# Second layer of a two-layer MLP chain: seven block products instead of eight in the second matmul, for three of a tile's four groups

## The chip, the cores and the metric

One core of a Trainium2 chip runs the kernel alone. The metric is device time in microseconds (us) of one execution. The kernel before was timed in three runs, and one further execution was profiled.

## The reference

Linear attention makes x of 4608 tokens by 512. Two MLP layers follow, each 512 to 2048 to 512; only their activations differ:

```python
x = attention(q, k, v)                     # 4608 x 512
h = x @ w_in;  r = np.maximum(h, 0.0)      # first layer, 512 x 2048
x = (r * r) @ w_out                        # 2048 x 512
h = x @ w_in;  g = h * np.cos(h)           # second layer
out = g @ w_out
```

All of it is float32. The kernel gets that accuracy from fp32r matmuls by splitting each operand into a high and a low part (`h` by a cast, `l` by a subtraction) and running three matmuls per product: high by high, high by low, low by high. The weights arrive as float64 words and are converted on the chip.

## The kernel before

**Two phases.** In the first (up to 497 us on the profile's clock) the attention runs, and beside it the first layer with its first 1024 hidden units, one chunk after the other (`run_chunks`). In the second, `run_slots` does the rest. Its unit is a **slot** `(m, t, q)`: layer m (0 or 1), token tile t (four of 1024 tokens and one of 512, each as two halves j of `ht` = 512 or 256 tokens) and group q of 512 hidden units. Layer 0 has two groups left per tile, layer 1 has four: 10 + 20 slots.

**First products of a slot.** `first_product` (L457) computes the 2 x 2 blocks of h from the 2 x 2 blocks of x and w_in in seven block products of 12 matmuls instead of eight (the Strassen-Winograd scheme), 84 matmuls with 512 columns (256 in the small tile). They go alternately to the PSUM tiles FA and FB; `keep` (ScalarE), `add` (VectorE) and `last` (ScalarE) drain them, each before the product after next may write the same tile. The seven combinations of x come from `x_block`, once per tile, those of w_in are made at conversion time and lie in DRAM (`wi_d`).

**Activation.** Layer 1 takes h times cos h in five steps, `cos_1` to `cos_5` (ScalarE, VectorE, ScalarE, ScalarE, VectorE), then `g_hi` (ScalarE) and `g_lo` (VectorE) split the result, block by block.

**Second products.** `second` (L555) multiplies g by w_out without block tricks. In layer 1 that is 96 matmuls of 512 columns per slot (48 in the small tile): 8 output units of 128 tokens, 4 chunks of 128 hidden units, three matmuls each. Four units share the PSUM tiles SA and SB (two banks each), and `drain` (L579) empties a tile into the SBUF tile `sum`: ScalarE copies for a tile's group 0, VectorE adds for the others. After the last group `sum` goes out.

**Order.** `run_slots` interleaves: after each first product matmul, as many second ones as are due. The second products of slot k start at position `k + LAG2` with LAG2 = 1.12, in units of one slot's 84 first matmuls. Loads, drains and activation steps are jobs at positions of their own (`at(pos(...), ...)`), and a scheduler of the framework orders the instructions of each engine from that. An engine works through its instructions in order.

**Buffers.** `w_p` holds 16 tiles of 4 KB per partition: loaded `wi` and `wo`, the `sum` tiles, and in the slots also the high parts `wh` of weights being converted (`conv_w`, L143). The pool `c` holds 18 tiles for h, y and g. All loads and stores of the slots are issued by SyncE.

**Conversion.** `load_w`/`conv_w` take 24 items of kind "out" (w_out, 8 of layer 0 and 16 of layer 1) and 24 of kind "pair" (w_in), on a timetable (`w_items`): the "out" items during the first phase, the 16 "pair" items of layer 1 between slots 0.5 and 8.4.

Of the kernel before, what the change touches and what calls it, by code (L numbers as in the profile page):

```python
# [8 lines left out]
F32 = mybir.dt.float32  # L9
# [13 lines left out]
def kernel(  # L23
# [77 lines left out]
    def as32(ap):  # L101
        return ap.bitcast(F32)
# [40 lines left out]
    def conv_w(kind, m, f, i):  # L143
        raw = raws.pop((kind, m, f, i))
        if kind == "pair":
# [10 lines left out]
            l = a.bitcast(F32R)[:, 1:]  # L156
            nc.scalar.copy(out=h, in_=a[:, 1:])  # L157
            nc.vector.tensor_tensor(out=l, in0=a[:, 1:], in1=as32(h[:]), op=ALU.subtract)
            q, pp = divmod(f - first_pair[m], 2)
            for k, x in enumerate((h[:], l)):  # L160
                nc.sync.dma_start(out=wi_d[m, q][:, :, k, pp, i, :], in_=as32(x))
# [383 lines left out]
    def sum_tile(k, n):  # L545
        m, t, q = slots[k]
        j, i = units(k)[2 * n]
        t0, ht = TILES[t]
        if q == 0:
            sums[m, t, n] = e = w_p.tile([P, 2, 512], F32, tag="w", name="sum")  # L550
            if m == 0:
                for b, s0, done, size in pieces(t0 + j * ht, ht, TOK):
                    nc.sync.dma_start(out=e[:, :, done:done + size], in_=p_d[b][:, i:i + 2, s0:s0 + size])

    def second(k, n):  # L555
        m, t, q = slots[k]
# [22 lines left out]
    def drain(k, n):  # L579
        m, t, q = slots[k]  # L580
        t0, ht = TILES[t]
        j, i = units(k)[2 * n]
        ps = psum[("SA", "SB")[n % 2]]
        e = sums[m, t, n]
        if m == 0:
            e, ps = e[:, :, :ht], ps[:, :, :ht]
        if q or m == 0:
# [3 lines left out]
        if q < groups_of[m][-1]:  # L591
            return
        if m == 0:
            nc.sync.dma_start(out=y_d[t][:, j, i:i + 2, :], in_=e)
        else:
            r = t0 + j * ht + i * P
            nc.sync.dma_start(out=out[r:r + 2 * P, :].rearrange("(a p) d -> p a d", p=P), in_=e)
# [11 lines left out]
    def pos(slot):  # L609
        return nA0 + slot + 0.002  # L610
# [18 lines left out]
    def outs_of(m, ps):  # L629
        return [("out", m, f, 1) for p in ps for f in (2 * p, 2 * p + 1)]  # L630

    def pairs_in(m, ps):
        return [("pair", m, p, i) for p in ps for i in range(2)]

    w_items, w_at = [], []
    for fs, n, step in ((range(2), -14, 0.1), (range(2, 6), -2.2, 0.7), (range(6, NH), 4, 0.8)):
# [37 lines left out]
    for k, (m, t, q) in enumerate(slots):  # L674
        if q == 0:
            for a in range(2):
                at(pos(k + (a - 3.6) * PH) if k else nA0 - 6, load_quads, m, t, a)
            for f, i in enumerate(ORDER):
                at(pos(k + (f - 1.9) * PH) if k or f > 2 else nA0 - 4 + f, x_block, k, i)
        for f, i in enumerate(ORDER):  # L680
            at(pos(k + (f - 2.7) * PH) if k or f > 2 else nA0 - 5 + f / 2, load_wi, k, i)
        for a, c in enumerate(CHUNKS):
            at(pos(k + LAG2 - 0.4 + a / 8), load_wo, k, c)
# [7 lines left out]
        chain = (cos_1, cos_2, cos_3, cos_4, cos_5, g_hi, g_lo) if m else (relu_1, relu_2, g_hi, g_lo)  # L691
# [3 lines left out]
        for n in range(len(units(k)) // 2):  # L695
# [24 lines left out]
            run_jobs(n + 0.5)  # L720

    def run_slots():
        seconds = [
            (k + LAG2 + n / len(units(k)) / 12, k, n)
            for k in range(len(slots))
            for n in range(12 * len(units(k)))
        ]
# [27 lines left out]
    with ExitStack() as early:  # L755
# [6 lines left out]
        with tc.tile_pool(name="att", bufs=1, side="right") as att_p:  # L762
# [64 lines left out]
```

## Time and profile before

| | us |
|---|---|
| median of 3 runs (lowest, highest) | 1623.52 (1622.73, 1629.05) |
| the profiled execution | 1623.71 |
| its span, first to last instruction | 1621.6 |
| TensorE (PE) busy | 1589.4 |
| VectorE (DVE) busy | 1056.2 |
| ScalarE (ACT) busy | 947.9 |
| GpSimd (POOL) busy | 81.3 |

The span is 2.1 us shorter than the execution's own time. "PEld" is the weight loading of TensorE, which runs beside the matmuls. Matmuls are pipelined: one is listed with 390 ns, while the next starts 0.23 us after it, so their rate is read from starts, not from durations. The layer-1 slots stand from about 872 us to the end; there TensorE never pauses until the last drain.

### The profile page before, as it was taken

To read this page: it belongs to the slowest core of one execution; us is meant where nothing else is said; L and a number is where in the kernel's file an instruction comes from. 1 tells how busy PE (TensorE), PEld (TensorE's weight loads), DVE (VectorE), ACT (ScalarE), POOL (GpSimd) and SP (SyncE) were. 2 spreads that over 40 slices of the span, in tenths; PEclk is the share of its full clock that TensorE was granted. 3 is DMA by queue.
4 is the path that set the end of the run, shared out by engine and by line. 5 is a ranking of instruction groups with operands and counts; after the bars stand their busy time and mean duration, and the time that the engine had idled before them with its cause. 6 is when DMAs were issued, how large, how long until landed. Compare 5 with 4: busy or idle time off the path is not lost.

```text
span 1621.6 us, 21070 instructions
## 1 busy us (share of the span) xinstructions
PE 1589.4 (98%) x7928; PEld 1305.7 (81%) x7928; DVE 1056.2 (65%) x1410; ACT 947.9 (58%) x1348; POOL 81.3 (5%) x74
## 2 busy tenths in 40 slices
PE   5999999999999999999999999999999999999998
PEld 4777777788887887778789888888888888888887
DVE  7967777787766867565536557645764576456645
ACT  6977777774436645554435656555655555555554
POOL 1102222232000000000000000000000000000000
PEclk9999999999999999999999999999999999999999
DMA  9855787554577988787778544644564455544682
GB/s 323 266 170 176 245 261 242 176 195 150 169 241 268 326 291 283 259 282 247 274 262 291 189 136 166 211 159 131 168 208 169 130 169 181 182 130 155 221 301 90
DMA packets 169572, 344.27 MB, mean 212 GB/s; under 512 B 15360, under 2 KB 92672, under 8 KB 169472
## 3 DMA queue, kind: packets, MB, share of 16 engines
q1 hardware_dynamic: 168704, 340.58, 63.2%
q0 software_dynamic: 768, 2.36, 0.4%
q8 instruction: 63, 1.03, 0.3%
q14 instruction: 37, 0.30, 0.1%
HBM read 270.53 MB, written 72.35 MB: 211 GB/s over the span
## 4 chain that ended last, share of the span: by engine, by line
PE 88%; DMA 5%; DVE 4%; ACT 2%; issue 1%; SPq 1%; POOL 0%; DVEq 0%; POOLq 0%
PE SB L572 17%; PE SA L572 17%; PE FA L467 15%; PE FB L467 15%; PE acc L386 10%; PE l L349 9%; DMA wi_d<-raw 1%; PE o L349 1%; DMA xraw<-x_d 1%; DMA wi<-wi_d 1%; PE ss L349 1%; DMA q<-in_qT 1%; DVE sum L588 1%; PE l L228 0%; PE o L262 0%
## 5 line engine op out<-in xcount | busy, mean ns | idle before, releaser
L467 PE MATMUL FA<-xh,wi 128*128 128x512 f32 (+1 forms) x840 | 304.0, 368 | 1.4 <-issue 1.3
L467 PE MATMUL FB<-xh,wi 128*128 128x512 f32 (+1 forms) x840 | 304.0, 368 | 0.0
L572 PE MATMUL SA<-wo,gh 128*128 128x512 f32 x576 | 223.1, 390 | 0.0
L572 PE MATMUL SB<-wo,gh 128*128 128x512 f32 x576 | 212.1, 390 | 0.0
L467 PEld LDWEIGHTS FA<-xh,wi 128*128 128x128 f32 x840 | 157.8, 188 | 30.6 <-issue 1.7
L508 ACT ACTIVATE y<-h,zerob 128x1024 int32<-128x1024 f32 (+1 forms) x80 | 85.4, 1067 | 164.3 <-DVE h L487 163.7
L467 PEld LDWEIGHTS FB<-xh,wi 128*128 128x128 f32 x840 | 157.8, 188 | 28.2 <-DVE h L491 0.2
L526 DVE SCALAR_TENSOR_TENSOR y<-y,h 128x1024 f32<-128x1024 f32 (+1 forms) x80 | 89.4, 1117 | 95.8 <-ACT y L522 95.8
L572 PEld LDWEIGHTS SB<-wo,gh 128*128 128x128 f32 x576 | 107.9, 188 | 21.9 <-ACT gh L532 0.2
L572 PEld LDWEIGHTS SA<-wo,gh 128*128 128x128 f32 x576 | 108.1, 188 | 21.2
L512 DVE SCALAR_TENSOR_TENSOR y<-y,h 128x1024 f32<-128x1024 int32 (+1 forms) x80 | 89.3, 1116 | 52.5 <-ACT y L508 51.8
L572 PE MATMUL SA<-gh,wo 128*128 128x512 f32 (+1 forms) x320 | 118.2, 372 | 5.0 <-ACT wh L157 2.7
L518 ACT ACTIVATE y<-y 128x1024 f32<-128x1024 f32 (+1 forms) x80 | 78.1, 976 | 62.8 <-DVE y L512 62.8
L536 DVE TENSOR_TENSOR gl<-y,gh 128x1024 fp32r<-128x1024 f32 (+1 forms) x80 | 89.3, 1116 | 38.4 <-ACT gh L532 38.4
L386 PE MATMUL acc<-gh,wh 128*128 128x512 f32 x288 | 113.6, 396 | 0.0
L386 PE MATMUL acc<-gl,wh 128*128 128x512 f32 x288 | 112.9, 392 | 0.0
L386 PE MATMUL acc<-gh,wl 128*128 128x512 f32 x288 | 112.6, 391 | 0.0
L572 PE MATMUL SB<-gh,wo 128*128 128x512 f32 (+1 forms) x320 | 111.5, 370 | 1.1 <-DVE sum L588 1.1
L572 PE MATMUL SB<-wo,gl 128*128 128x512 f32 x288 | 112.4, 390 | 0.0
L572 PE MATMUL SA<-wo,gl 128*128 128x512 f32 x288 | 112.3, 390 | 0.0
L467 PE MATMUL FA<-xl,wi 128*128 128x512 f32 (+1 forms) x300 | 110.5, 368 | 0.0
L467 PE MATMUL FB<-xl,wi 128*128 128x512 f32 (+1 forms) x300 | 110.3, 368 | 0.0
(156 smaller groups left out, 3282.5 us busy)
## 6 DMA issues: line engine op xcount, KB each, us to landing
wi<-wi_d SPq DMA_DIRECT2D x210, 512.0 KB, 4.6
wo<-wo_d SPq DMA_DIRECT2D x120, 512.0 KB, 4.6
kvld<-in_kv SPq DMA_DIRECT2D x32, 512.0 KB, 6.8
raw<-in_wA SPq DMA_DIRECT2D x24, 512.0 KB, 5.3
wi_d<-wh SPq DMA_DIRECT2D x24, 448.0 KB, 3.3
wi_d<-raw SPq DMA_DIRECT2D x24, 448.0 KB, 3.9
q<-in_qT SPq DMA_DIRECT2D x32, 288.0 KB, 4.1
p_d<-ev SPq DMA_DIRECT2D x18, 512.0 KB, 3.7
```

The source lines that it names most:

```text
L349: nc.tensor.matmul(ps, a[:, 0, cs], m[:], start=(c == 0 and k == 0), stop=(c == NKC - 1 and k == 2))
L386: nc.tensor.matmul(o, a[:, cs], m[:], start=(f == 0 and n == 0), stop=(f == NH - 1 and n == 2), skip_group_check=True)
L467: nc.tensor.matmul(ps[:, pp, :], a, b, start=(i in (0, 1, 2) and n == 0), stop=(n == 5), skip_group_check=True)
L508: nc.scalar.activation(out=y.bitcast(I32), in_=hs[k, b], func=AF.Identity, bias=zerob)
L512: nc.vector.scalar_tensor_tensor(out=y, in0=y.bitcast(I32), scalar=-1.0, in1=hs[k, b], op0=ALU.mult, op1=ALU.add)
L518: nc.scalar.activation(out=y, in_=y, func=AF.Sin, scale=math.pi)
L526: nc.vector.scalar_tensor_tensor(out=y, in0=y, scalar=-2.0 * math.pi, in1=hs.pop((k, b)), op0=ALU.add, op1=ALU.mult)
L536: nc.vector.tensor_tensor(out=l, in0=ys.pop((k, b)), in1=as32(h), op=ALU.subtract)
L572: nc.tensor.matmul(ps, lhs, rhs, start=(a == 0 and (x, y) == (0, 0)), stop=last, skip_group_check=True)
L588: nc.vector.tensor_tensor(out=e, in0=ps, in1=e, op=ALU.add)
```

## The change

For groups 0, 1 and 2 of every layer-1 tile (`seven`) the second products become seven block products too. The block form has half as many output columns: each matmul has 256 columns (`second_product`), 24 of them per product, 168 per slot (84 in the small tile) where 96 (48) stood. Group 3 keeps `second`.

- The seven combinations of g are made by `s_block` (four subtractions, then seven casts and seven subtractions, where four of each stood).
- The seven combinations of w_out are made at conversion time (kind "seven") and stored in `ws_d`; `load_ws` loads seven tiles of 512 KB per slot in the place of four `wo`. 12 "out" items go, 12 "seven" items come: 8 in the first phase, 4 among the 16 "pair" items, whose stretch now ends at slot 9.
- Partial products accumulate in SA and SB as in the first products; `drain_product` empties one after each product into four `sum` tiles per token tile (four ScalarE copies and three VectorE adds in group 0, seven VectorE adds in groups 1 and 2). Group 3's drains are split into two adds of 512 elements, since `sum` is laid out by column halves.
- LAG2 goes from 1.12 to 1.25. The `wh` of conversions in the slots come from pool `c` instead of `w_p`; in the first phase they come in two halves from `temp`.

```diff
+    seven = {(1, q) for q in range(NP - 1)}
+    ws_d = {k: dram.tile([P, NPR, 2, 2, 2, P], F32, name=f"ws_d{k[1]}") for k in sorted(seven)}
...
-            p_h, tag = (pools["h"], "w") if pools["h"] is w_p else (pools["h"], "x")
-            h = p_h.tile([P, NPR, P], F32R, tag=tag, name="wh")
...
+            where = [n for n in ("c", "x") if n in pools]
+            if where:
+                parts = [(0, 8, pools[where[0]].tile([P, 8, P], F32R, tag=where[0], name="wh"))]
+            else:
+                parts = [(o, o + 4, temp([P, 4, P], F32R, "wh")) for o in (0, 4)]
...
+    S_ORDER = (0, 2, 3, 4, 5, 1, 6)
...
+    def s_block(k, i):
+        m, t, q = slots[k]
+        b11, b12, b21, b22 = (ys.get((k, b)) for b in ((0, 0), (0, 1), (1, 0), (1, 1)))
...
+        if i == 2:
+            ys[k, "t1"] = minus(t_tile(k, F32, "t"), b12, b11)
+        if i == 3:
+            ys[k, "t2"] = minus(t_tile(k, F32, "t"), b22, ys[k, "t1"])
...
+        gs[k, i] = h, l = [t_tile(k, F32R, f"g{n}") for n in "hl"]
+        nc.scalar.copy(out=h, in_=src)
+        nc.vector.tensor_tensor(out=l, in0=src, in1=as32(h), op=ALU.subtract)
...
+    def s_bank(k, i):
+        return psum[("SA", "SB")[(k + (i in (1, 2, 4))) % 2]]
...
+                    nc.tensor.matmul(
+                        ps[:, b, :],
+                        g[y][:, pp, b * P:(b + 1) * P],
+                        w[:, x, pp, :, :].rearrange("p i n -> p (i n)"),
+                        start=(i in (0, 1, 2) and n == 0 and b % 2 == 0),
+                        stop=(n == 5),
+                        skip_group_check=True,
+                    )
...
+    def drain_product(k, i):
+        m, t, q = slots[k]
+        ps, d, j = blocks_of(t, s_bank(k, i)), *SUM_OF[i]
+        if q == 0 and i in (0, 2, 3, 6):
+            sums[t, d, j] = e = w_p.tile([P, 2, 512], F32, tag="w", name="sum")
+            nc.scalar.copy(out=blocks_of(t, e), in_=ps)
         else:
-            nc.scalar.copy(out=e, in_=ps)
...
+            e = blocks_of(t, sums[t, d, j])
+            nc.vector.tensor_tensor(out=e, in0=ps, in1=e, op=ALU.add)
...
-    LAG2 = 1.12
+    LAG2 = 1.25
...
+        if (m, q) in seven:
+            for f, i in enumerate(S_ORDER):
+                at(pos(k + LAG2 + (f - 2.7) * PH), load_ws, k, i)
+                at(pos(k + LAG2 + (f - 1.6) * PH), s_block, k, i)
+        else:
+            for a, c in enumerate(CHUNKS):
+                at(pos(k + LAG2 - 0.4 + a / 8), load_wo, k, c)
```

**TensorE, a stretch in the middle of layer 1.** In these rows `wi` and `x` belong to first products, `wo`/`ws` and `g` to second ones. Before:

```order
L467 MATMUL FA_5629<-xl_10864,wi_10831 128x512
L572 MATMUL SB_5632<-wo_10681,gl_10549 128x512
L467 MATMUL FA_5629<-xh_10862,wi_10831 128x512
L572 MATMUL SB_5632<-wo_10681,gh_10548 128x512 x2
L467 MATMUL FA_5629<-xh_10862,wi_10831 128x512
```

With the change:

```order
L657 MATMUL SA_5650<-ws_10925,gl_10985 128x256
L488 MATMUL FA_5648<-xh_9917,wi_10890 128x512
L657 MATMUL SA_5650<-ws_10925,gh_10984 128x256 x2
L488 MATMUL FB_5649<-xh_9979,wi_10944 128x512
L657 MATMUL SA_5650<-ws_10925,gl_10985 128x256
```

Between two first matmuls of 512 columns there now stand two second ones of 256, where one of 512 stood most of the time.

**VectorE, the fourth slot of the second layer-1 tile.** L588 and L680 drain second products, L512/L526 and L533/L547 are cosine steps, L536, L557 and L640 make low parts of g, L422/L441 and L438/L457 are the next tile's `x_block`, L622 the new combinations. Before, the first rows after the last `add` of the slot ahead; 26 rows stand between that add and the next of its kind:

```order
L512 SCALAR_TENSOR_TENSOR y_10381<-y_10381,h_10370 128x1024
L536 TENSOR_TENSOR gl_10392<-y_10343,gh_10391 128x1024
L526 SCALAR_TENSOR_TENSOR y_10381<-y_10381,h_10370 128x1024
L588 TENSOR_TENSOR sum_10001<-SA_5631,sum_10001 128x1024
L512 SCALAR_TENSOR_TENSOR y_10422<-y_10422,h_10412 128x1024
L536 TENSOR_TENSOR gl_10435<-y_10381,gh_10434 128x1024
L588 TENSOR_TENSOR sum_10063<-SB_5632,sum_10063 128x1024
```

With the change, from the same place:

```order
L547 SCALAR_TENSOR_TENSOR y_10888<-y_10888,h_10871 128x1024
L640 TENSOR_TENSOR gl_10932<-y_10635,gh_10931 128x1024
L533 SCALAR_TENSOR_TENSOR y_10942<-y_10942,h_10922 128x1024
L680 TENSOR_TENSOR sum_10449<-SB_5651,sum_10449 128x1024
L547 SCALAR_TENSOR_TENSOR y_10942<-y_10942,h_10922 128x1024
L640 TENSOR_TENSOR gl_10985<-y_10740,gh_10984 128x1024
L680 TENSOR_TENSOR sum_10398<-SA_5650,sum_10398 128x1024
L533 SCALAR_TENSOR_TENSOR y_10995<-y_10995,h_10976 128x1024
L622 TENSOR_TENSOR t_11037<-y_10942,y_10740 128x1024
L622 TENSOR_TENSOR y_10942<-y_10888,y_10942 128x1024
```

Between the same two adds there are now 33 rows. Counted the same way, the four slots of a full tile had 17, 17, 26 and 23 and have 26, 28, 33 and 30 (in the first and the last of these four are 128x512).

**SyncE, the loads of the last, small tile.** Before:

```order
L446 DMA wi_13083<-wi_d1_1_96 128x1024
L451 DMA wo_13104<-wo_d1_3_110 128x1024
L446 DMA wi_13121<-wi_d1_1_96 128x1024
L597 DMA out_0<-sum_12039 128x2x512
L597 DMA out_0<-sum_12116 128x2x512
L451 DMA wo_13143<-wo_d1_0_107 128x1024
```

With the change:

```order
L467 DMA ws_14999<-ws_d2_101 128x1024
L462 DMA wi_15014<-wi_d1_3_98 128x1024
L467 DMA ws_15040<-ws_d2_101 128x1024
L462 DMA wi_15055<-wi_d1_3_98 128x1024
L467 DMA ws_15078<-ws_d2_101 128x1024
L462 DMA wi_15094<-wi_d1_3_98 128x1024
```

Per slot there are now fourteen such loads where there were eleven.

## Rows read from the trace of the kernel before

**Rows 1.** The page, part 1: TensorE's busy time.

```profile
span 1621.6 us, 21070 instructions
PE 1589.4 (98%) x7928; PEld 1305.7 (81%) x7928; DVE 1056.2 (65%) x1410; ACT 947.9 (58%) x1348; POOL 81.3 (5%) x74
```

**Rows 2.** The page, part 2: granted TensorE clock in 40 slices.

```profile
PEclk9999999999999999999999999999999999999999
```

**Rows 3.** The page, part 4: the chain that ended last, by engine.

```profile
PE 88%; DMA 5%; DVE 4%; ACT 2%; issue 1%; SPq 1%; POOL 0%; DVEq 0%; POOLq 0%
```

**Rows 4.** Windows: busy us (x instructions) per engine, clock, DMA share, GB/s.

```profile
0.00:497.00 497.00, 476.62 (x2720) 376.07 (x2720) 376.45 (x699) 324.61 (x684) 81.30 (x74) 1.00 0.66 215
497.00:872.00 375.00, 368.23 (x1733) 306.97 (x1734) 238.60 (x307) 197.91 (x217) 0.00 (x0) 1.00 0.85 287
872.00:1604.00 732.00, 732.00 (x3424) 612.95 (x3423) 433.20 (x397) 421.08 (x441) 0.00 (x0) 1.00 0.53 176
...
997.00:1372.00 375.00, 375.00 (x1656) 310.41 (x1655) 232.91 (x197) 216.62 (x210) 0.00 (x0) 1.00 0.50 165
1552.00:1598.00 46.00, 46.00 (x290) 41.15 (x289) 22.74 (x33) 26.64 (x43) 0.00 (x0) 1.00 0.68 234
834.00:868.00 34.00, 34.00 (x243) 31.93 (x242) 19.97 (x23) 17.45 (x27) 0.00 (x0) 1.00 0.97 352
```

**Rows 5.** Timeline, TensorE, layer 0's small tile: start us, us, instruction.

```profile
848.90 0.28 PE L572 MATMUL SA<-gh,wo 128*128 128x256 f32 x1
...
852.98 0.28 PE L572 MATMUL SB<-gh,wo 128*128 128x256 f32 x1
```

**Rows 6.** Timeline, VectorE, six instructions back to back in layer 1.

```profile
1222.60 1.22 DVE L526 SCALAR_TENSOR_TENSOR y<-y,h 128x1024 f32<-128x1024 f32 x1 [1.09 <-ACT y L522]
...
1228.32 1.23 DVE L526 SCALAR_TENSOR_TENSOR y<-y,h 128x1024 f32<-128x1024 f32 x1
```

**Rows 7.** Groups by line and form, VectorE: count, busy us, mean ns, idle before.

```profile
L124 DVE SCALAR_TENSOR_TENSOR e<-raw,e 128x512 uint32<-128x512 uint32 x64 | 45.0, 702 | 8.9 <-ACT e L117 8.6
L153 DVE TENSOR_TENSOR raw<-raw 128x128 f32<-128x128 f32 x96 | 26.8, 320 | 1.3
L158 DVE TENSOR_TENSOR raw<-raw,wh 128x896 fp32r<-128x896 f32 x24 | 26.1, 1086 | 1.7 <-ACT wh L157 1.1
L588 DVE TENSOR_TENSOR sum<-SA,sum 128x512 f32<-128x512 f32 x4 | 2.8, 689 | 3.7 <-PE SA L572 3.6
```

**Rows 8.** Waits, VectorE, 900 to 1600 us: us in total, times, longest.

```profile
DVE y L526 <- ACT y L522: 93.9, 55, 3.0
DVE y L512 <- ACT y L508: 50.4, 48, 1.9
...
DVE gl L536 <- ACT gh L532: 37.5, 39, 1.1
```

**Rows 9.** Waits, TensorE, 497 to 872 us (layer 0's slots).

```profile
PE SA L572 <- ACT wh L157: 2.7, 2, 2.2
PE SA L572 <- DVE sum L588: 2.3, 2, 1.7
...
PE SB L572 <- DVE sum L588: 1.1, 2, 0.6
```

**Rows 10.** Timeline, TensorE, after the longest pause of layer 0's slots.

```profile
687.28 0.76 PE L572 MATMUL SA<-gh,wo 128*128 128x512 f32 x1 [2.25 <-ACT wh L157]
687.85 0.63 PE L572 MATMUL SA<-gl,wo 128*128 128x512 f32 x1
```

**Rows 11.** Window behind that pause, columns as in rows 4.

```profile
687.30:691.00 3.70, 3.70 (x10) 2.93 (x11) 3.70 (x5) 1.02 (x1) 0.00 (x0) 0.56 0.88 269
```

**Rows 12.** Waits, VectorE, whole span.

```profile
DVE e L116 <- DMA raw<-in_wB: 39.5, 11, 6.6
```

**Rows 13.** DMA issues: count, KB each, us to landing.

```profile
wi<-wi_d SPq DMA_DIRECT2D x210, 512.0 KB, 4.6
```

**Rows 14.** The page, part 5: TensorE's weight loads of first products.

```profile
L467 PEld LDWEIGHTS FA<-xh,wi 128*128 128x128 f32 x840 | 157.8, 188 | 30.6 <-issue 1.7
```

More of the change, by code (lines that the diff above doesn't have):

```diff
@@ L129, in load_w @@
     def load_w(kind, m, f, i):
-        if kind == "pair":
+        if kind == "seven":
+            raw = conv_p.tile([P, 4, P, 2], U32, tag="raw", name="raw")
+            for df, places in ((0, (1, 0)), (1, (2, 3))):
+                src = (wA, wB)[m][2 * f + df, :, 1, :].rearrange("p (c n) -> p c n", n=2 * P)
+                for d, place in enumerate(places):
+                    nc.sync.dma_start(out=raw[:, place].rearrange("p n two -> p (n two)"), in_=src[:, 2 * d + i, :])
+        elif kind == "pair":
             raw = conv_p.tile([P, 4, P, 2], U32, tag="raw", name="raw")
@@ L144, in conv_w @@
         raw = raws.pop((kind, m, f, i))
-        if kind == "pair":
+        if kind in ("pair", "seven"):
             w, ef = words(raw, [P, 4, P])
@@ L153, in conv_w @@
                 nc.vector.tensor_tensor(out=a[:, o], in0=a[:, x], in1=a[:, y], op=op)
-            p_h, tag = (pools["h"], "w") if pools["h"] is w_p else (pools["h"], "x")
-            h = p_h.tile([P, NPR, P], F32R, tag=tag, name="wh")
-            l = a.bitcast(F32R)[:, 1:]
-            nc.scalar.copy(out=h, in_=a[:, 1:])
-            nc.vector.tensor_tensor(out=l, in0=a[:, 1:], in1=as32(h[:]), op=ALU.subtract)
-            q, pp = divmod(f - first_pair[m], 2)
-            for k, x in enumerate((h[:], l)):
-                nc.sync.dma_start(out=wi_d[m, q][:, :, k, pp, i, :], in_=as32(x))
+            where = [n for n in ("c", "x") if n in pools]
[3 more added lines that the diff above has]
+                parts = [(o, o + 4, temp([P, 4, P], F32R, "wh")) for o in (0, 4)]
+            q, pp = divmod(f - first_pair[m], 2)
+            dst = (wi_d if kind == "pair" else ws_d)[m, q][:, :, :, pp, i, :]
+            l = a.bitcast(F32R)
+            for o, end, t in parts:
+                lo = max(o, 1)
+                h = t[:, lo - o:end - o]
+                nc.scalar.copy(out=h, in_=a[:, lo:end])
+                nc.vector.tensor_tensor(out=l[:, lo:end], in0=a[:, lo:end], in1=as32(h), op=ALU.subtract)
+                nc.sync.dma_start(out=dst[:, lo - 1:end - 1, 0, :], in_=as32(h))
+            nc.sync.dma_start(out=dst[:, :, 1, :], in_=as32(l[:, 1:]))
             return
@@ L446, in load_wi, with load_ws @@
         nc.sync.dma_start(out=as32(w[:]), in_=wi_d[m, q][:, W_OF[i]])
+    def load_ws(k, i):
+        m, t, q = slots[k]
+        wo[k, i] = w = w_p.tile([P, 2, 2, 2, P], F32R, tag="w", name="ws")
+        nc.sync.dma_start(out=as32(w[:]), in_=ws_d[m, q][:, W_OF[i]])
     def load_wo(k, c):
@@ L550, in sum_tile @@
             sums[m, t, n] = e = w_p.tile([P, 2, 512], F32, tag="w", name="sum")
-            if m == 0:
-                for b, s0, done, size in pieces(t0 + j * ht, ht, TOK):
-                    nc.sync.dma_start(out=e[:, :, done:done + size], in_=p_d[b][:, i:i + 2, s0:s0 + size])
+            for b, s0, done, size in pieces(t0 + j * ht, ht, TOK):
+                nc.sync.dma_start(out=e[:, :, done:done + size], in_=p_d[b][:, i:i + 2, s0:s0 + size])
     def second(k, n):
@@ L583, in drain @@
         ps = psum[("SA", "SB")[n % 2]]
-        e = sums[m, t, n]
         if m == 0:
-            e, ps = e[:, :, :ht], ps[:, :, :ht]
-        if q or m == 0:
+            e, ps = sums[m, t, n][:, :, :ht], ps[:, :, :ht]
             nc.vector.tensor_tensor(out=e, in0=ps, in1=e, op=ALU.add)
-        else:
-            nc.scalar.copy(out=e, in_=ps)
[L591 to L597, printed above, removed]
+            if q == groups_of[m][-1]:
+                nc.sync.dma_start(out=y_d[t][:, j, i:i + 2, :], in_=e)
@@ new lines, in drain, with minus @@
+            return
+        for d in range(2):
+            e = blocks_of(t, sums[t, d, j])[:, i:i + 2, :]
+            nc.vector.tensor_tensor(out=e, in0=ps[:, :, 2 * P * d:2 * P * (d + 1)], in1=e, op=ALU.add)
+            if i + 2 == ht // P:
+                dst = out[t0 + j * ht:t0 + (j + 1) * ht, 2 * P * d:2 * P * (d + 1)]
+                nc.sync.dma_start(out=dst.rearrange("(b p) n -> p b n", p=P), in_=blocks_of(t, sums[t, d, j]))
+    def s_block(k, i):
+        m, t, q = slots[k]
+        b11, b12, b21, b22 = (ys.get((k, b)) for b in ((0, 0), (0, 1), (1, 0), (1, 1)))
+        def minus(out, x, y):
+            nc.vector.tensor_tensor(out=out, in0=x, in1=y, op=ALU.subtract)
+            return out
+        if i == 2:
+            ys[k, "t1"] = minus(t_tile(k, F32, "t"), b12, b11)
+        if i == 3:
+            ys[k, "t2"] = minus(t_tile(k, F32, "t"), b22, ys[k, "t1"])
+        src = {
+            0: lambda: b11,
+            1: lambda: b21,
+            2: lambda: ys[k, "t1"],
+            3: lambda: ys[k, "t2"],
+            4: lambda: b22,
+            5: lambda: minus(b12, b22, b12),
+            6: lambda: minus(b21, b21, ys[k, "t2"]),
+        }[i]()
+        gs[k, i] = h, l = [t_tile(k, F32R, f"g{n}") for n in "hl"]
+        nc.scalar.copy(out=h, in_=src)
+        nc.vector.tensor_tensor(out=l, in0=src, in1=as32(h), op=ALU.subtract)
@@ new lines, in blocks_of, with second_product @@
+    def blocks_of(t, x):
+        return x.rearrange("p c n -> p (c n)").rearrange("p (b n) -> p b n", n=2 * P)[:, :TILES[t][1] // P]
+    def s_bank(k, i):
+        return psum[("SA", "SB")[(k + (i in (1, 2, 4))) % 2]]
+    def second_product(k, i):
+        m, t, q = slots[k]
+        ps = blocks_of(t, s_bank(k, i))
+        w, g = wo.pop((k, i)), gs.pop((k, i))
+        nb = TILES[t][1] // P
+        for b in range(nb):
+            n = 0
+            for pp in range(2):
+                for x, y in ((0, 0), (0, 1), (1, 0)):
+                    nc.tensor.matmul(
[6 more added lines that the diff above has]
+                    )
+                    n += 1
+                    if n == 6 and b == nb - 1:
+                        drain_product(k, i)
+                    yield
@@ L630, in outs_of, with pairs_in @@
         return [("out", m, f, 1) for p in ps for f in (2 * p, 2 * p + 1)]
-    def pairs_in(m, ps):
-        return [("pair", m, p, i) for p in ps for i in range(2)]
+    def pairs_in(m, ps, kind="pair"):
+        return [(kind, m, p, i) for p in ps for i in range(2)]
     w_items, w_at = [], []
@@ L640 @@
     for new, n0, n1 in (
-        (outs_of(0, range(NP, 2 * NP)) + outs_of(1, range(2 * NP)), 13, nAtt + 1),
+        (outs_of(0, range(NP, 2 * NP)) + outs_of(1, range(6, 8)) + pairs_in(1, range(4), "seven"), 13, nAtt + 1),
         (pairs_in(0, range(NP, 2 * NP)), nAtt + 1, nA0 - 6),
-        (pairs_in(1, range(2 * NP)), pos(0.5), pos(8.4)),
+        (pairs_in(1, range(2 * NP)) + pairs_in(1, range(4, 6), "seven"), pos(0.5), pos(9)),
     ):
@@ L681 @@
             at(pos(k + (f - 2.7) * PH) if k or f > 2 else nA0 - 5 + f / 2, load_wi, k, i)
-        for a, c in enumerate(CHUNKS):
-            at(pos(k + LAG2 - 0.4 + a / 8), load_wo, k, c)
+        if (m, q) in seven:
[5 more added lines that the diff above has]
+                at(pos(k + LAG2 - 0.4 + a / 8), load_wo, k, c)
         at(pos(k + 1 * PH), keep, k, "m1", 0)
@@ L690 @@
         at(pos(k + 7 * PH), last, k)
-        chain = (cos_1, cos_2, cos_3, cos_4, cos_5, g_hi, g_lo) if m else (relu_1, relu_2, g_hi, g_lo)
+        chain = (cos_1, cos_2, cos_3, cos_4, cos_5) + (() if (m, q) in seven else (g_hi, g_lo)) if m else (relu_1, relu_2, g_hi, g_lo)
         for b, f in BLOCKS.items():
@@ L694 @@
                 at(pos(k + (f + 0.25 * (a + 1)) * PH), fn, k, b)
-        for n in range(len(units(k)) // 2):
+        for n in range(0 if m else 4):
             at(pos(k + LAG2 - 0.2 + 2 * n / len(units(k))), sum_tile, k, n)
@@ L722, in run_slots @@
     def run_slots():
[L723 to L726, printed above, removed]
+        size = [
+            7 * 6 * TILES[t][1] // P if (m, q) in seven else 12 * len(units(k)) for k, (m, t, q) in enumerate(slots)
         ]
+        seconds = [k + LAG2 + n / size[k] for k in range(len(slots)) for n in range(size[k])]
         firsts = [(k, i) for k in range(len(slots)) for i in ORDER]
         steps1 = (x for k, i in firsts for x in first_product(k, i))
-        steps2 = (x for s0, k, n in seconds if n % 48 == 0 for x in second(k, n // 48))
+        todo = [
+            (second_product, k, i) if slots[k][0::2] in seven else (second, k, i)
+            for k in range(len(slots))
+            for i in (S_ORDER if slots[k][0::2] in seven else range(len(units(k)) // 4))
+        ]
+        steps2 = (x for fn, *a in todo for x in fn(*a))
         nf, ns = 12 * len(firsts), 0
@@ L735, in run_slots @@
             run_jobs(nA0 + here)
-            while ns < len(seconds) and seconds[ns][0] <= here:
+            while ns < len(seconds) and seconds[ns] <= here:
                 next(steps2)
@@ L773 @@
             run_chunks(0, nAtt)
-        pools["x"] = pools["h"] = ctx.enter_context(tc.tile_pool(name="xb", bufs=13, side="left"))
+        pools["x"] = ctx.enter_context(tc.tile_pool(name="xb", bufs=13, side="left"))
         banks["l"] = ["l0", "l1", "o", "ss"]
```

3 lines of the change are left out of this document (2 added, 1 removed).

## The prediction

> **What bounds the kernel now.** I read the page first. TensorE is busy 1589.4 of 1621.6 us [rows 1], at the upper of its two clock levels in all 40 slices [rows 2], and it carries 88% of the chain that ended last [rows 3]. Then the windows [rows 4]: in the first phase it is busy 476.62 of 497 us, in layer 0's slots 368.23 of 375, in layer 1's slots 732 of 732. The change is in layer 1. There TensorE alone sets the time, while VectorE works 433 us and ScalarE 421 us of 732 and the DMA engines half the time. So a matmul taken away there gives its time back, and anything that makes TensorE wait there is new.
>
> **TensorE's work.** Of second products, 1296 matmuls of 512 columns go (12 groups in full tiles by 96, 3 in the small one by 48), and 2268 of 256 come (12 by 168, 3 by 84). A matmul of 512 takes 375 us / 1656 = 0.2264 us of TensorE in layer 1 [rows 4]. For 256 columns the nearest stretch is layer 0's small tile, where first and second products both have 256: 35 matmuls start from 848.90 to 852.98, so 4.08 / 34 = 0.1200 us [rows 5]. The mixed stretch of layer 1's small tile agrees: of its 290 matmuls in 46 us [rows 4], 84 in 132 or 184.5 have 256 columns; at 0.2264 the other 105.5 take 23.9 us, which leaves 0.120 each. So 1296 x 0.2264 = 293.4 us go and 2268 x 0.1200 = 272.2 come: **21.2 us saved**, 1.6 per full slot (21.7 to 20.2) and 0.8 per small one. The columns shrink by an eighth, the time by only 7%, since each matmul costs some 13 ns beyond its columns and there are more of them. Bounds: at exactly half of 0.2264 it would be 36.7 us; at 0.129 nothing. I take 0.1200 because it is measured with these shapes; an error of 2 ns is 4.5 us.
>
> The Trainium skill, "TensorE: Matmul & The Clock Gate", section "Wait — 56ns, not 53.3ns?", gives a fixed cost of only about 2.5 ns per matmul. An estimate from that page is 109 ns for 256 columns and 216 for 512, hence 32 us saved and a time near 1597. The rows show about 13 ns at both sizes, so the rows decide.
>
> **VectorE.** Back to back, its 1024-element instructions start (1228.32 - 1222.60) / 5 = 1.144 us apart [rows 6], and a 512-element one lasts 0.69 [rows 7]. With the numbers of instructions per slot of a full tile in the order (26, 28, 33, 30, with four of the first and of the last at 512) that is 27.9, 32.0, 37.8 and 32.5 us of work. TensorE's slot is then 84 x 0.2264 = 19.0 us of first products and 20.2 of second, 39.2 us, and 40.7 where group 3's are the second ones. So VectorE goes from about 59% of the layer to about 82%, and to 96% in the fourth slot. That hides as long as its waits for ScalarE don't add up: now it waits 93.9 + 50.4 + 37.5 = 181.8 us for ScalarE in layer 1 [rows 8], about 10 us per full slot (16 full slots and 4 half ones). Much of this is slack: with more work queued, other instructions stand between the links of a chain. If VectorE is late all the same, the drains of FA, FB, SA and SB are late, TensorE's next matmul into that tile waits, and all matmuls behind it too, first ones included. A product of 24 small matmuls with 12 first ones between takes 24 x 0.12 + 12 x 0.2264 = 5.6 us, which is what a drain may be late in seven-product slots. I charge one late drain per tile, in the fourth slot. The price is that of layer 0's slots, where six waits on second products' tiles cost 2.7 + 2.3 + 1.1 = 6.1 us, 1.0 each [rows 9]: **5 us** for five tiles. Bounds: 0, and the 39 us worked out below.
>
> **ScalarE** gets three casts more per slot, about 45 us in a layer in which it has 311 us free [rows 4]; TensorE covers it, and without this cover it would be 45 us.
>
> **Conversions.** 12 items become dearer. One "seven" item costs VectorE at most five instructions of 0.70, four of 0.32 and 1.09, 5.9 us [rows 7]; eight in the first phase are 47 us before the twelve "out" items that go are counted, and VectorE idles 120 us there. Four come into layer 0's slots, 24 us against 136 idle [rows 4]. I cost them, the extra 36 small raw loads of SyncE, the 12 subtractions less on GpSimd and the move of `wh` from one pool to another at nothing: TensorE covers them. But layer 0's slots already have the 6.8 us of TensorE pauses, with VectorE held up by late raw weights for up to 6.6 us [rows 12], and conversions get denser there while `wi` and `wo` get buffers back. Either way at most 6.8: gone, or doubled.
>
> **Loads.** Per slot 14 loads of 512 KB take the place of 11, 7.3 MB in 39.2 us. That is 187 GB/s in a layer that now draws 176 with a DMA share of 0.53 [rows 4]. `load_ws` stands 2.7/7 of a slot ahead of use, 15 us, against 4.6 us to landing [rows 13]. Only the small tile is tight: 7.3 MB in 20.2 us are 363 GB/s, and the fastest stretch shows 352 at a share of 0.97 [rows 4]. At 352 the two slots with 14 loads each would be 0.7 us late: 0 to 1.4 us, and I take 0, since the lead of 7.8 us covers it.
>
> **LAG2 and the drains of group 3** change no TensorE work; the later start leaves 2.5 us more second products behind the last first one, which covers the last cosine chain. 0.
>
> **Sum.** The profiled execution took 1623.7 us: 1623.7 - 21.2 + 5 = **1607.5 us**. The median of the runs is 0.2 us less, which changes nothing.
>
> **Rivals.**
>
> 1. No new waits, and layer 0's pauses go too: 1623.7 - 21.2 - 6.8 = 1596 (1602.5 with the pauses left). For: a drain may be 5.6 us late, where the two drains of `second` leave about 2.5 us between a tile's last matmul and the next use. Against: 96% of VectorE in one slot.
>
> 2. **VectorE becomes the bound in the fourth slot of each tile**, and the kernel gets slower. If all 10 us of waits for ScalarE stay, the slot takes VectorE 47.8 us, 8.6 beyond TensorE's 39.2; four full tiles and a half-sized one make 39 us: 1623.7 - 21.2 + 39 = 1641.5. It decides from 21.2 / 4.5 = 4.7 us per full tile, that is when 6.1 us of waits remain in that slot. Long pauses cost double: after TensorE had stood 2.25 us, matmuls of 512 started 0.43 us apart [rows 10], at a granted clock of 0.56 over 3.7 us, so mostly the 1.2 GHz level [rows 11], which is another 1.6 us each. For: the queue is in order and the chain crosses engines four times. Against: the slots before and after have 7 and 8 us to spare, and part of the lateness can be made up there.
>
> 3. Transfers eat the gain: the small tile's loads cost 1.4 us and layer 0's pauses double. 1607.5 + 1.4 + 6.8 = 1615.7, on the edge of what counts as faster. For: DMA share 0.85 there, 0.97 at the end. Against: TensorE lost nothing in that 0.97 stretch.
>
> 4. Matmuls of 256 don't take half the time, since each one loads weights for the same 128 columns: if loads of 188 ns [rows 14] set the pace, a slot would take 168 x 0.188 = 31.6 us instead of 21.7, 134 us in all: 1758. Against: in rows 5 matmuls start 0.120 apart, with such a load for each. The Trainium skill, on the same page, section "Back-to-back issue gap", has sustained 81 ns for 128 columns and 131 for 512. An estimate on a line between them, 98 ns for 256, would make a full slot 3.9 us dearer; but 512 columns stand at 226 here, so that rule doesn't fit this kernel.
>
> **Chances.** About 0.5%, 8 us, is what a measurement of this kernel can tell from no change; so faster is below 1615.4 and slower above 1631.6. The forecast (TensorE still the bound, a few microseconds of waits) gets 0.60, of which 0.52 lie below 1615.4. Rival 1 gets 0.13, all faster; rival 2 gets 0.15, of which 0.09 slower and 0.06 between; rival 3 gets 0.10, half and half; rival 4 gets 0.02, slower. Faster 0.70, the same 0.19, slower 0.11. The range goes from rival 1's 1596 up to 1626, which takes in rival 3 and the lower part of rival 2 and leaves out about 0.15.
>
> **What would show it.** Right: second products of 256 columns starting about 0.120 us apart among 0.226 for the first ones; layer 1 shorter by 16 to 21 us; TensorE's waits there only on L680 or L508, about 1 us each, in fourth slots; VectorE about 80% busy in layer 1. Wrong: small matmuls at 0.125 or more; waits of several microseconds on VectorE in every tile, with a lower granted clock behind them; or waits on `ws`, which I hold for hidden.

## The result and the profile after

The changed kernel takes **1602.2 us** (median of four runs, 1599.5 to 1602.7) beside 1624.1 for the kernel before in the same call: a ratio of 0.9856 [0.9833, 0.988]. That is 21.9 us less; 1607.5 had been forecast, with a range of 1596 to 1626. The profiled execution took 1602.58 us.

The page of the changed kernel, parts 1, 2, 4 and 6:

```profile
span 1600.8 us, 23614 instructions
...
PE 1568.4 (98%) x8900; PEld 1331.2 (83%) x8900; DVE 1219.8 (76%) x1650; ACT 984.2 (61%) x1403; POOL 64.8 (4%) x62
...
PEclk8999999999999999999999999999999999999999
...
PE 77%; DMA 9%; DVE 8%; ACT 3%; issue 2%; SPq 1%; POOL 0%; DVEq 0%; POOLq 0%; ACTq 0%
...
wi<-wi_d SPq DMA_DIRECT2D x210, 512.0 KB, 4.8
ws<-ws_d SPq DMA_DIRECT2D x105, 512.0 KB, 4.3
```

TensorE's busy time fell by 21.0 us [rows 1], the span by 20.8. The program issues 972 matmuls more and is shorter. VectorE went from 65% to 76% of the span. The chain that ended last now passes more often through VectorE and DMA [rows 3]. That alone says little, since it can follow either of two engines that are both busy; the windows say where TensorE stood.

Windows of the changed kernel, as in rows 4 (its last stretch of layer 1 ends 21 us sooner):

```profile
0.00:497.00 497.00, 477.19 (x2725) 376.83 (x2726) 372.53 (x730) 322.30 (x683) 64.76 (x62) 0.99 0.68 218
497.00:872.00 375.00, 368.65 (x1726) 305.98 (x1725) 257.16 (x343) 205.54 (x226) 0.00 (x0) 1.00 0.88 296
872.00:1583.00 711.00, 711.00 (x4403) 639.38 (x4402) 583.38 (x568) 453.06 (x489) 0.00 (x0) 1.00 0.64 214
...
1153.00:1192.00 39.00, 39.00 (x225) 34.30 (x224) 37.12 (x33) 27.78 (x28) 0.00 (x0) 1.00 0.57 179
...
1540.00:1560.00 20.00, 20.00 (x169) 20.00 (x168) 17.51 (x28) 13.68 (x24) 0.00 (x0) 1.00 1.03 418
```

In layer 1 TensorE still works without a gap, 711 of 711 us, while VectorE works 583 of them, 82% (59% before). The fourth row is a fourth slot of a full tile: VectorE is busy 37.1 of its 39 us, and TensorE doesn't wait.

TensorE's waits in the changed kernel, first in layer 0's slots, then from 872 us to the end:

```profile
PE SA L592 <- DVE sum L606: 4.6, 5, 2.2
PE FA L488 <- ACT m L502: 0.9, 1, 0.9
PE SB L592 <- DVE sum L606: 0.5, 2, 0.2
PE FA L488 <- ACT u L502: 0.2, 1, 0.2
...
PE SA L592 <- ACT y L543: 0.8, 1, 0.8
```

Layer 0's pauses are 6.4 us in all (375 - 368.65) where they were 6.8, at other places: the longest is now one of 2.2 us at 542, no longer the one at 687 [rows 9, 10]. In the whole of layer 1 there is one wait, 0.8 us, at the very end.

VectorE's waits in the changed kernel, 900 to 1580 us:

```profile
DVE y L547 <- ACT y L543: 38.7, 29, 2.2
DVE gl L640 <- ACT gh L639: 35.2, 31, 2.8
...
DVE y L533 <- ACT y L529: 1.9, 3, 0.8
```

These three are the waits for ScalarE that came to 181.8 us before [rows 8]; now they come to 75.8. With more work queued, VectorE is doing something else for most of the time that ScalarE works.

TensorE's timeline in the changed kernel, in a full tile (start us, us, instruction):

```profile
1002.26 0.39 PE L488 MATMUL FA<-xraw,wi 128*128 128x512 f32 x1
1002.49 0.28 PE L657 MATMUL SB<-ws,gh 128*128 128x256 f32 x1
1002.61 0.28 PE L657 MATMUL SB<-ws,gl 128*128 128x256 f32 x1
1002.73 0.40 PE L488 MATMUL FA<-xh,wi 128*128 128x512 f32 x1
```

Starts 0.23 us apart behind a matmul of 512 columns and 0.12 behind one of 256. A steady full tile gives this more exactly. The same VectorE instruction (the first `xl` subtraction of a tile's split) comes every 163.21 us in the kernel before and every 158.46 in the changed one. Windows of one such tile, the kernel before:

```profile
997.66:1160.87 163.21, 163.21 (x722) 135.12 (x721) 98.46 (x85) 94.09 (x91) 0.00 (x0) 1.00 0.51 168
```

and the changed kernel:

```profile
991.49:1149.94 158.45, 158.45 (x938) 140.55 (x937) 131.26 (x118) 101.15 (x100) 0.00 (x0) 1.00 0.62 203
```

So **4.75 us per full tile**, and 4.5 tiles (the small one counted half) make 21.4.

### The profile page after: what moved, and what is told of

It reads as the page before. It is cut to its first block, busy times and chain, and to the rows that moved or that the text cites. A ratio compares the mean times of both kernels' runs of the same rounds, so it can differ in the third digit from the quotient of the medians.

```text
span 1600.8 us, 23614 instructions
## 1 busy us (share of the span) xinstructions
PE 1568.4 (98%) x8900; PEld 1331.2 (83%) x8900; DVE 1219.8 (76%) x1650; ACT 984.2 (61%) x1403; POOL 64.8 (4%) x62
## 4 chain that ended last, share of the span: by engine, by line
PE 77%; DMA 9%; DVE 8%; ACT 3%; issue 2%; SPq 1%; POOL 0%; DVEq 0%; POOLq 0%; ACTq 0%
PE FA L488 13%; PE FB L488 13%; PE acc L401 10%; PE SA L657 9%; PE l L364 8%; PE SB L657 8%; PE SA L592 6%; PE SB L592 6%; DMA wi_d<-raw 2%; DMA raw<-in_wB 1%; DMA xraw<-x_d 1%; PE o L364 1%; DVE sum L606 1%; PE ss L364 1%; DMA x_d<-xo 1%
## 5 line engine op out<-in xcount | busy, mean ns | idle before, releaser
L657 PE MATMUL SA<-ws,gh 128*128 128x256 f32 x792 | 196.9, 280 | 0.0
L657 PE MATMUL SB<-ws,gh 128*128 128x256 f32 x720 | 180.1, 280 | 0.0
L657 PEld LDWEIGHTS SA<-ws,gh 128*128 128x128 f32 x792 | 147.8, 188 | 14.4
L657 PEld LDWEIGHTS SB<-ws,gh 128*128 128x128 f32 x720 | 134.8, 188 | 13.5
L547 DVE SCALAR_TENSOR_TENSOR y<-y,h 128x1024 f32<-128x1024 f32 (+1 forms) x80 | 89.3, 1116 | 46.2 <-ACT y L543 46.2
L592 PE MATMUL SB<-gh,wo 128*128 128x512 f32 (+1 forms) x320 | 117.2, 370 | 0.5 <-DVE sum L606 0.5
L657 PE MATMUL SA<-ws,gl 128*128 128x256 f32 x396 | 111.0, 280 | 0.0
L640 DVE TENSOR_TENSOR gl<-y,gh 128x1024 fp32r<-128x1024 f32 (+1 forms) x75 | 83.5, 1114 | 30.0 <-ACT gh L639 30.0
L657 PE MATMUL SB<-ws,gl 128*128 128x256 f32 x360 | 100.9, 280 | 0.0
L364 PE MATMUL l<-xh,wh 128*128 128x512 f32 x240 | 96.7, 403 | 1.1 <-ACT xh L333 0.9
```

The costliest lines, as they stand in the source:

```text
L364: nc.tensor.matmul(ps, a[:, 0, cs], m[:], start=(c == 0 and k == 0), stop=(c == NKC - 1 and k == 2))
L547: nc.vector.scalar_tensor_tensor(out=y, in0=y, scalar=-2.0 * math.pi, in1=hs.pop((k, b)), op0=ALU.add, op1=ALU.mult)
L592: nc.tensor.matmul(ps, lhs, rhs, start=(a == 0 and (x, y) == (0, 0)), stop=last, skip_group_check=True)
L640: nc.vector.tensor_tensor(out=l, in0=src, in1=as32(h), op=ALU.subtract)
L657: nc.tensor.matmul(ps[:, b, :], g[y][:, pp, b * P:(b + 1) * P], w[:, x, pp, :, :].rearrange("p i n -> p (i n)"), start=(i in (0, 1, 2) and ...
```

## The experiments

**What a matmul costs.** Three runs change the mix of 512 and 256 columns, and one takes the lag and the pool alone. `e2_halves` is the kernel before with each second product of groups 0 to 2 in two halves:

```
for cols in (slice(0, 256), slice(256, 512)) if m and q < 3 else ...:
    nc.tensor.matmul(ps[:, cols], lhs, rhs[:, cols], ...)
```

> The kernel before, with each 512-column second product of groups 0 to 2 of layer 1 issued as two of 256 columns, 1296 matmuls more and the same columns. Theory (0.2264 us for 512 columns, 0.1200 for 256, so some 13 ns per matmul beside its columns): 1296 x (0.2400 - 0.2264) = +17.6 us, 1641.7. Rival, the fixed cost of 2.5 ns per matmul that the Trainium skill states: +3 us, 1627. Rival, weight loads of 188 ns set the pace: 1296 x (0.376 - 0.2264) = +194 us, 1818.

Measured: 1643.3 us, ratio 1.0116 [1.0095, 1.0138]. `e4_all_groups` is the changed kernel with all four groups in seven products:

```
-    seven = {(1, q) for q in range(NP - 1)}
+    seven = {(1, q) for q in range(NP)}
```

(and group 3's results stored from `drain_product`, its weights converted in place of the remaining "out" items).

> The change with all four groups of each layer-1 tile in seven products; of w_out of layer 1 nothing is converted in plain form any more. VectorE then has 140 us of work per full tile against TensorE's 157, and 37.6 and 39.9 in two of its slots against 39.2. Theory (VectorE's load costs nothing while lateness within a tile can be made up): 4 x 1.56 + 0.8 = 7 us below the changed kernel, 1595. Rival 2 of the prediction (a slot of VectorE at its limit holds TensorE up): TensorE waits of several us per tile in layer 1 and no gain over the changed kernel, 1602 or more.

Measured: **1595.2 us**, 0.9814 [0.9797, 0.983]. It beats the changed kernel by 7 us, as expected. `e3_one_group` has seven products in group 0 alone (with the conversions that go with it, on the timetable of the kernel before):

```
-    seven = {(1, q) for q in range(NP - 1)}
+    seven = {(1, q) for q in range(1)}
```

> The change with only group 0 of each layer-1 tile in seven products. Theory: a third of the matmul saving, 21.2 / 3 = 7.1 us below before, 1617. Rival (LAG2 and pool carry a part that doesn't scale with the groups): well below 1617, 1605 to 1612. Rival (VectorE costs back part of each group): a third of the measured 22 us as well, but with TensorE waits on drains in layer 1.

Measured: 1622.5 us, 0.9988 [0.9978, 0.9998]: a miss by 5.5 us. `e1_lag_pool` is the kernel before with

```
-    LAG2 = 1.12
+    LAG2 = 1.25
```

and with `wh` in the chains' pool, as in the change.

> The kernel before with the change's LAG2 = 1.25 and with the converted weights' high parts in pool c, and with nothing of the seven products. Theory (the gain is TensorE's shorter second products alone): no matmul changes, so 1624 us, at most 5 us off to either side by pauses of layer 0 that move. Rival (the later start and the freed w buffers carry part of the gain): 5 to 10 us faster than before, 1614 to 1619.

Measured: 1627.1 us, 1.0015 [1.0003, 1.0028]: the two edits bring no gain by themselves, but cost 2.7 us. They have no part in the gain of a tile either, since a steady one takes 163.22 us where the kernel before takes 163.21:

```profile
993.32:1156.54 163.22, 163.22 (x722) 135.17 (x721) 98.65 (x83) 94.24 (x92) 0.00 (x0) 1.00 0.50 168
```

Windows of one steady tile each, `e2_halves`:

```profile
998.85:1166.48 167.63, 167.63 (x1010) 149.22 (x1009) 98.64 (x84) 94.09 (x91) 0.00 (x0) 1.00 0.49 164
```

`e3_one_group`, and its layer 0:

```profile
998.20:1160.10 161.90, 161.90 (x794) 136.91 (x793) 110.27 (x106) 96.27 (x95) 0.00 (x0) 1.00 0.53 179
...
497.00:872.00 375.00, 363.45 (x1691) 301.02 (x1690) 238.56 (x306) 195.69 (x215) 0.00 (x0) 1.00 0.84 277
```

`e4_all_groups`, and one of its fourth slots:

```profile
989.15:1145.95 156.80, 156.80 (x1010) 142.30 (x1009) 141.53 (x124) 103.40 (x103) 0.00 (x0) 1.00 0.67 215
...
1153.00:1192.00 39.00, 39.00 (x253) 35.37 (x252) 38.75 (x35) 28.19 (x29) 0.00 (x0) 1.00 0.66 203
```

TensorE is busy all of each tile, so its price list can be read off. A tile of the kernel before has 336 first and 384 second products of 512 columns, 163.21 / 720 = 0.2267 us each. With that price for 512 columns, one of 256 costs:

| kernel | 512 / 256 columns in a tile | tile, us | one of 256, us |
|---|---|---|---|
| before | 720 / 0 | 163.21 | |
| e2_halves | 432 / 576 | 167.63 | 0.1210 |
| e3_one_group | 624 / 168 | 161.90 | 0.1217 |
| changed | 432 / 504 | 158.45 | 0.1201 |
| e4_all_groups | 336 / 672 | 156.80 | 0.1200 |

So 0.120 to 0.122 in four mixes. The price that weight loads would set (rival 4) falls with `e2_halves`, where 1818 us would have come.

Two parts of the miss of `e3_one_group` can be told. It has the lag and the pool of `e1_lag_pool`, which ran 2.7 us over the kernel before. Its tile saves 1.31 us and not 1.56, since its few small matmuls cost 0.1217: 4.5 x 1.31 = 5.9 us. From 1627.1 that gives 1621.2, and 1.3 us remain open. Its profile shows 11.5 us of pauses in layer 0, but the profiled execution (1626.7) was the longest of its ten, 4.2 us above the median; what the pauses were at the median isn't shown.

**How much more VectorE can take.** In the changed kernel the low part of the first four (`e5_twice_4`) or all seven (`e6_twice_7`) combinations of a slot is computed twice:

```
+        for _ in range(2 if S_ORDER.index(i) < 4 else 1):
             nc.vector.tensor_tensor(out=l, in0=src, in1=as32(h), op=ALU.subtract)
```

> The changed kernel, in which VectorE computes the low part of the first four of a slot's seven combinations twice (60 more instructions of 1.22 or 0.68 us, 67 us of VectorE work; no result is changed). Theory, that what VectorE has to do in a whole tile decides, and that a slot with more work than TensorE gives it is made up in its neighbours: 145 us of a tile's 157, so 0 to 3 us over the changed kernel's 1602.2, and TensorE waits at second products for less than 3 us in layer 1. Rival, that each fourth slot must hold its own work (42 us in 39): some 3.5 us for each of four tiles, 1616, with waits of TensorE once per tile.

Measured: 1607.2 us (1605.4 to 1607.8), 0.9892 [0.9878, 0.9907]: 5.0 over the changed kernel, 2 more than the theory allowed and 9 less than the rival.

> The same with all seven low parts twice (105 more instructions, 117 us). Theory: 156 us of a tile's 157 on VectorE, at the edge: 0 to 8 us over 1602.2. Rival of the slot as the bound: 46 us in 39 for the fourth, some 7 us per tile, 1630 and more. If both theories are wrong and VectorE had no part in the time at all, 1602.

Measured: 1641.6 us, 1.0108 [1.0093, 1.0123]: the theory's 0 to 8 us fall here, and the rival's size is right.

A tile of `e5_twice_4`, and TensorE's wait in such tiles (872 us to the end):

```profile
1005.16:1164.95 159.79, 159.10 (x938) 140.55 (x937) 144.43 (x131) 100.35 (x101) 0.00 (x0) 1.00 0.62 201
...
PE SA L592 <- DVE sum L681: 2.1, 3, 0.7
```

A tile of `e6_twice_7`, TensorE's waits in it, and the window behind its pause:

```profile
1017.25:1182.50 165.25, 161.00 (x938) 142.10 (x937) 154.30 (x139) 100.92 (x101) 0.00 (x0) 0.99 0.59 195
...
PE SA L658 <- DVE gl L641: 3.0, 1, 3.0
PE SA L658 <- ACT y L529: 1.0, 1, 1.0
...
1025.30:1028.30 3.00, 2.98 (x14) 2.98 (x15) 3.00 (x3) 2.70 (x3) 0.00 (x0) 0.52 0.03 5
```

With VectorE at 144 us of a tile (90%) there is one late drain, 0.7 us, in each of three tiles, and a tile is 1.3 us longer. With 154 us of work for what had been a tile of 158 (97%) TensorE waits 4.2 us per tile; a granted clock of 0.52 over the 3 us behind the pause, mostly the 1.2 GHz level, costs part of the rest, and a tile is 6.8 us longer. Lateness is thus made up between slots while a tile as a whole has room (`e4_all_groups`: 38.75 of 39 us in one slot, and no wait of TensorE there), and no longer when it has next to none. One rival is not separated from this: the doubled subtraction also stands in the path from a combination to its matmuls, and the longest wait of `e6_twice_7` is for just such a low part (`gl`).

**Layer 0's pauses**, 6 to 7 us in the kernel before as in the changed one, were a term of the prediction that could have gone either way. In VectorE's queue the first step of a weight conversion (`e<-raw`) waits for its raw load, and TensorE's drains stand behind it. The kernel before shows it at its longest pause: VectorE had stood 6.62 us for a raw load, and the drain that followed (`sum`) ended at 687.19, 0.09 us before TensorE's next matmul (the row in [rows 10] names ScalarE's `wh`, which was done at 687.01).

```profile
682.95 0.43 DVE L116 TENSOR_SCALAR e<-raw 128x512 uint32<-128x512 uint32 x1 [6.62 <-DMA raw<-in_wB]
...
685.97 1.22 DVE L588 TENSOR_TENSOR sum<-SA,sum 128x1024 f32<-128x1024 f32 x1
```

`e7_raw_pool` moves the raw loads of layer 1's weights that run beside layer 0 to GpSimd's queue, `e8_all_raw` does the same to `e4_all_groups`:

```
-   nc.sync.dma_start(out=raw..., in_=src...)
+   (nc.gpsimd if m else nc.sync).dma_start(out=raw..., in_=src...)
```

> The changed kernel; the loads of layer 1's quantized weights that run beside layer 0 are issued by GpSimd's queue, not SyncE's. Theory, that the 6.4 us of pauses of TensorE in layer 0 come from VectorE's wait for these loads, which stand behind other transfers in SyncE's queue: pauses below 2 us, 1595 to 1599. Rival, that the loads are late because the memory is busy: pauses and time stay, 1600 to 1604.

> Seven products for all four groups (run before at 1595.2) with the same move of the raw loads to GpSimd's queue. Theory: the pauses of layer 0 (5.9 us in that run's profile) go: 1589 to 1592. Rival: 1595 as before.

Measured: 1643.7 and 1643.1 us, 1.0116 [1.0095, 1.0138] and 1.0106 [1.0079, 1.0133]: 41 and 48 us slower, far outside both expectations. `e7_raw_pool`, layer 0: window, waits of VectorE and TensorE:

```profile
497.00:872.00 375.00, 339.36 (x1450) 274.89 (x1449) 234.38 (x322) 183.42 (x196) 28.71 (x44) 0.96 0.78 259
...
DVE e L118 <- DMA raw<-in_wB: 88.8, 17, 10.0
...
PE SA L594 <- DVE sum L608: 21.6, 8, 6.3
PE SB L594 <- DVE sum L608: 8.8, 3, 8.4
```

The pauses grew from 6.4 to 35.6 us, and VectorE's waits for raw loads from 32.5 [compare rows 12] to 88.8. The chain is confirmed (late raw loads hold VectorE, VectorE holds the drains), but leaving SyncE's queue did not make the loads sooner. The changed kernel's own trace says why a crowded SyncE queue is unlikely as the reason. There this queue stands at the raw loads until the store of an earlier chunk has landed and its raw buffer is free (waits of SyncE's queue and of VectorE, 497 to 872 us):

```profile
SPq L142 <- DMA wi_d<-raw: 25.8, 13, 2.9
...
DVE e L118 <- DMA raw<-in_wB: 32.5, 13, 6.4
```

So `e9_own_low` to `e11_one_own_low` give the low part a buffer of its own, in the changed kernel, in `e4_all_groups` and in `e3_one_group`:

```
-            l = a.bitcast(F32R)
+            l = pools["c"].tile([P, 8, P], F32R, tag="c", name="wl") if "c" in pools else a.bitcast(F32R)
```

> The changed kernel; beside layer 0, the low part of a converted weight chunk goes to a buffer of its own in the chains' pool and not back into the raw buffer, so that the next raw load waits for VectorE's last step alone and not for the store to land (3.2 to 3.5 us later in the runs so far). Theory, that layer 0's pauses come from the ring of two raw buffers (last step, store, landing, load, landing, first step of the chunk after next, which stands 4 to 10 places behind in VectorE's queue): VectorE's waits for raw loads fall from 32.5 us to below 15, TensorE's pauses in layer 0 from 6.4 to 1 to 3 us, 1596 to 1600. Rival, that the loads are late in themselves: no change, 1602.

> Seven products for all four groups with the same buffer for the low part. Theory: 1595.2 less 3 to 5, 1590 to 1592. Rival: 1595.

> Seven products for group 0 alone (1622.5 when it ran, 1617 expected) with the same buffer for the low part. Its profile had 11.5 us of pauses in layer 0 where the kernel before has 6.8, and four full tiles of layer 1 in 635.4 us where the kernel before takes 641.9. Theory, that the 5 us missing then were those pauses and the saving of a group is 7.1 us: pauses of 2 to 4 us, 1613 to 1617, and the four tiles again at 634 to 636. Rival, that one group alone saves only some 2 us in layer 1: 1618 and more, and the four tiles at 640.

Measured: 1602.7 us (0.9865 [0.9845, 0.9885]), 1597.1 (0.9826 [0.9812, 0.9839]) and 1621.4 (0.9982 [0.9973, 0.9991]). Nothing is gained. `e9_own_low`, layer 0:

```profile
497.00:872.00 375.00, 367.75 (x1726) 306.10 (x1725) 256.24 (x342) 205.16 (x226) 0.00 (x0) 1.00 0.88 296
...
DVE e L118 <- DMA raw<-in_wB: 31.5, 12, 4.8
```

SyncE's wait for the stores is gone and the loads go out sooner (one at 565.21 us where the changed kernel has it at 569.88), but VectorE waits 31.5 us as before. So the wait for a free raw buffer is not by itself the reason. It isn't cleared in full either, since in the program's order `e<-raw` moved up with its load (570.9 where it was 575.2): it stands 2 to 16 places behind the last step of an earlier chunk, with or without the new buffer. My reading is that the order is laid out for loads that land sooner than the 3 to 7 us they take; that is argued and not shown, and a later place for that step was not tried. `e11_one_own_low` has pauses of 8.7 us where `e3_one_group` had 11.5, with the same tile of 161.9 us, and its median is 1.1 us lower. Its theory (1613 to 1617) fell too, since the pauses stayed.

**The lag once more.** `e12_all_early` is `e4_all_groups` with the lag of the kernel before:

```
-    LAG2 = 1.25
+    LAG2 = 1.12
```

> Seven products for all four groups, with the second products 1.12 slots behind the first as in the kernel before, not 1.25 (5 us earlier). Theory, that the 2.4 us by which the lag and the pool alone ran longer come from the lag, as pauses elsewhere: 1592 to 1594. Rival 1, that they are no part of the lag: 1595 as with 1.25. Rival 2, that combinations and their halves need the later start: TensorE waits on second products in layer 1, 1598 and more.

Measured: 1595.4 us, 0.9828 [0.9815, 0.9842], a steady tile again 156.80 us: no gain from the earlier start. That speaks against the lag as the source of the 2.7 us of `e1_lag_pool`, but neither of that run's two edits was tried alone in the kernel before, so they stay unexplained. At 1.12 the program writes the difference t1 of a slot 0.001 slots ahead of `cos_5` of a block that it reads, so t1 and what is made of it, the output too, lack that block's last step; the instructions are the same in number and size, and the time can be read. The change needs the later start for its order, not for its speed.

## Why the prediction came out as it did

- **TensorE's work**: right. 21.2 us were forecast; tiles show 21.4, the busy time 21.0 [compare rows 1]. The 0.1200 us read from layer 0's small tile [rows 5] held in layer 1 (0.1201). `e2_halves` tests the fixed part alone. There, 1296 matmuls become 2592, and 19 us come where 13 ns for each of 1296 give 17. An estimate from the 2.5 ns that the Trainium skill, "TensorE: Matmul & The Clock Gate", section "Wait — 56ns, not 53.3ns?", states is 3 us, a time of 1627; the measurement, 1643, decides against it for this kernel.
- **VectorE's load**: right. 130.2 us per tile were added up from the order, 131.3 were measured; 37.8 in the fourth slot, 37.1 measured; 82% of the layer both times.
- **The 5 us for late drains**: wrong, and nearly the whole error. "I charge one late drain per tile, in the fourth slot. The price is that of layer 0's slots ..." In layer 1 there was no late drain of that kind at all, and 0.8 us of waiting. The price came from a stage in which VectorE's queue stands behind raw weight loads, as the longest of the six waits and `e7_raw_pool` show; layer 1's slots have none. The reason against a wait was in the text ("much of this is slack") and was given too little weight: the waits for ScalarE fell from 181.8 to 75.8 us. The drain that I charged does exist, 0.7 us per tile, but only with 13 us more work in a tile (`e5_twice_4`).
- **Rival 2**: VectorE can become the bound, but over a whole tile and not within one slot: between 90 and 97% of a tile in these runs. The changed kernel is at 83% (131.3 of 158.5), `e4_all_groups` at 90% without a wait in the tile.
- **Rival 1** in its weaker form, no new waits and layer 0's pauses left, gave 1602.5: that is what came. I had given rival 1 0.13.
- **ScalarE, conversions, loads, the lag**: nothing that these runs show in the changed kernel, as said; the 2.7 us that the lag and the pool cost in `e1_lag_pool` were not foreseen. ScalarE worked 453 us of 711; the pauses went from 6.8 to 6.4; the loads took 4.3 and 4.8 us against a lead of 15. The bound of 352 GB/s for the small tile was too low: 418 GB/s moved from 1540 to 1560, with TensorE busy throughout. So rival 3 had no ground.
- **Signs**: starts 0.12 apart among 0.23, VectorE near 80%, layer 1's four full tiles 20.0 us shorter (the first product of layer 1 of 512 columns to that of its small tile: 641.88 and 621.87). The expected waits on L680 or L508 didn't come.

## What to carry to other kernels

Price a changed matmul by the pitch of the same shape in a stretch where the engine never stops, and check it by dividing a steady period by its matmuls. Before charging waits to an engine that gets more work, ask which period must hold the sum: here a slot could be 99% full without loss, since the queue made up the lateness in its neighbours, while a whole tile at 97% cost 6.8 us. And take the price of a wait only from a stage whose queue holds the same kind of blocker.

## What the runs showed of the hardware

- The core's transfers reached 418 GB/s at a DMA share of 1.03 in a stretch of 20 us, above the 352 seen before [rows 4], without delaying a matmul.
- The same raw loads, issued by GpSimd, took 1.45 us to issue for a pair and landed after 4.8 us (median), against 0.90 and 4.1 from SyncE:

`e7_raw_pool`, GpSimd:

```profile
589.56 1.45 POOL L142 DMA_DIRECT2D raw<-in_wB  x2 [15.50 <-DMA wi_d<-raw]
```

and the changed kernel, SyncE:

```profile
569.88 0.90 SPq L142 DMA_DIRECT2D raw<-in_wB  x2
```

In `e7_raw_pool` layer 0 (its first matmul to the first one of 512 columns in layer 1) took 408.0 us where the changed kernel takes 367.7: 29 of the 40 us are pauses, and the others stand beside a granted clock of 0.96 in the window. Why about 1 us more per pair of loads cost that much is not settled.
